# Decoding the first weight matrix without ScalarE and GpSimd, folding key blocks the other way, and a new order of every step

## Chip, cores and metric

The kernel runs on one core of one Trainium2 chip. The metric is device time in microseconds (us) of one execution, lower is better. The engines are TensorE (PE in the rows; PEld is its weight load), VectorE (DVE), ScalarE (ACT), GpSimd (POOL) and SyncE (SP, which here issues nearly all DMAs). Engines run their own queues in order and wait for each other through semaphores.

## The reference

Attention with a sliding window and four sink keys over batch 4, 8 heads, 768 positions and head dimension 64, then a gated layer of width 512 on the joined heads:

```python
scores = (q @ k.T) / sqrt(64)                # per batch and head
keep = (key < 4) | (0 <= query - key < 128)  # sinks, or inside the window
a = softmax(where(keep, scores, -1e9))
x = (a @ v), heads joined to width 512
gate_pre[t] = sum over 5 taps k of conv_w[k] * x[t - 4 + k]
out = (sigmoid(gate_pre) * (x @ w_val)) @ w_out
```

The weights w_val, w_out and conv_w come as float64 and are read as pairs of 32-bit words.

## The kernel before

**Steps of attention.** A step s is one of 24: a batch (4), a third of the positions p (3, 256 queries each) and a half of the heads qd (2). Each step has two units of scores g. `scores` (L376) multiplies 32 queries by the keys of their window in small tiles of TensorE (L396, 64 rows by 32 columns, eight tiles at a time) into one of two pairs of PSUM banks. The keys are laid out in blocks of 64, with the 4 sink keys behind each (HB = 68 columns), and a unit's row holds 200 columns for each of two key positions c: older block, sinks, middle block, sinks, newest block. Since the window is 128 wide, of the older and the newest block exactly one is valid at each place; `copy_predicated` (L401) folds the newest block into the older one's columns, so that the softmax runs over 132 columns instead of 200. For p = 0 the mask of the sequence's start is added while the maximum is taken (L410); for the others a plain maximum (L405) does. `exps` (L414) takes the exponentials on ScalarE, `recip` and `normalise` (L425, L430; five GpSimd operations) divide by the sums, `probs_t` (L449) and `sinks_t` (L462) transpose on TensorE, `probs_x`, `probs_y` and `sinks_e` bring the result to SBUF, `values` and `sinks` (L507, L522) multiply by V into the two banks xv.

**The gated layer.** Every two steps make 256 positions m (12 of them). `x_high`, `x_copy`, `x_low` (L540, L531, L548) split x into a high and a low part; `conv_last` (GpSimd) and `conv` (VectorE, L557, eight operations for each step) add the five taps, `gate` takes the tanh. `val` (L572) multiplies by w_val in three products (L581, 12 matmuls of 256 columns), `gated`, `gated_h`, `gated_l` multiply with the gate and split again, `outp` (L612) multiplies by w_out (L634, 6 matmuls of 512 columns each), `store` and `send` write 128 positions out. For the first m (those under `COPIES`) `val_copy` (L584) copies the product out of its bank to SBUF first, and `gated` reads the copy.

**Decoding of weights.** `_decode` (L124) turns float64 words of one quarter of a matrix (128 x 512) into a high and a low float32 part. `bias`, `bits` and `high` make the high part (ScalarE, VectorE, ScalarE); `power` gives the exponent e (L152, VectorE). `share` scales the low words on ScalarE (L160) and multiplies them by e on GpSimd (L161). `total` adds the three parts on TensorE (L182 to L184), `low` copies the result out (L187). The two last quarters of w_out (`CUT`) take another way.

**Banks.** Two PSUM banks ac (`homes`, L221) serve the decoding, the transposes of the sinks, `val` and `outp` in turn; a step that takes one (`homes.pop`) waits until the step that gave it back has read it. `busy` (L225) is a filler: it multiplies zeros n times in such a bank, so that TensorE works while it has nothing else.

**What sets the order.** `ORDER` (L36) is a table of names, a step's name and its number (s0.4 is unit 0 of the scores of step 4, wvc.0 the third stage of the first quarter of w_val, fill.5 five multiplications of zeros). `banded` runs through it once; the instructions stand on each engine's queue, SP's DMAs too, in exactly that order:

```python
    with tc.manual_schedule():
        for n in ORDER.split():
            f, args = events[n]
            f(*args)
```

The functions that the change touches, as they are in the kernel before:

Of the kernel before, what the change touches and what calls it, by code (L numbers as in the profile page):

```python
# [37 lines left out]
wva.1 kq.1 wvb.1 e0.0 blanks wva.2 wvb.2 vv.0 e1.0 wvf.0 fill.10 s1.1 wvc.2 wvc.1 rec.0 norm.0 wvd.1 e1.1 s0.1
fill.4 fill.7 kq.2 s1.2 wol.0 woa.0 wve.1 sv.0 e0.1 e1.2 wob.0 woc.0 wol.2 tx.0 fill.6 px.0 sk.0 py.0 rec.1
ts.0 wod.0 s0.2 vl.0 woe.0 wvl.3 wva.3 norm.1 wvb.3 kq.3 e0.2 s0.3 wof.0 wvf.1 si.0 xc.0 tx.1 px.1 fill.6 c4.0  # L40
kq.5 wvc.3 rec.2 norm.2 xh.0 wvd.2 hd.0 c0.0 wvd.3 e0.3 wve.2 c1.0 py.1 wol.3 wol.1 woa.1 wve.3 vv.1 wob.1
wvf.3 sv.1 tx.2 py.2 px.2 s1.3 xl.0 sk.1 ts.1 wod.1 wvf.2 kq.4 vl.1 si.1 xc.1 c4.1 sk.2 ts.2 kq.6 hd.1 woc.1
s0.4 xh.1 vv.2 woe.1 c0.1 e1.3 rec.3 woa.3 th.0 vv.5 e0.4 xl.1 v0.0 v1.0 c1.1 y0.0 wob.3 woa.2 norm.3 g0.0
wod.3 h0.0 vl.2 wob.2 th.1 s1.4 e1.4 l0.0 v2.0 v3.0 woe.3 woe.2 y1.0 g1.0 vv.6 tx.3 px.3 si.2 xc.2 hd.2 wof.1
h1.0 s0.6 o2.0 o0.0 rec.4 xh.2 py.3 c4.2 c0.2 l1.0 wof.2 s0.5 c1.2 s1.6 kq.7 wod.2 e0.6 wof.3 o1.0 t0.0 o3.0
norm.4 sk.3 e0.5 vv.3 ts.3 t1.0 xl.2 vl.3 si.3 xh.3 xc.3 hd.3 xl.3 c4.3 sk.4 th.2 s1.5 ts.4 tx.4 sv.6 px.4
e1.5 kq.8 c0.3 scalars d0.0 py.4 rec.5 v0.1 v1.1 y0.1 c1.3 e1.6 rec.6 v2.1 norm.5 g0.1 th.3 h0.1 v3.1 vv.4
y1.1 vl.4 tx.5 d1.0 kq.9 si.4 g1.1 l0.1 px.5 s1.8 sk.5 hd.4 xc.4 ts.5 o0.1 h1.1 c4.4 o2.1 xh.4 c0.4 warm_up
c1.4 py.5 l1.1 e1.8 o3.1 t1.1 s0.7 s1.7 vl.5 xl.4 norm.6 kq.10 tx.6 e0.7 si.5 sk.6 py.6 px.6 ts.6 xc.5 xh.5
o1.1 hd.5 e1.7 xl.5 s0.9 rec.7 t0.1 s0.8 v0.2 c4.5 c0.5 v1.2 th.4 kq.12 g0.2 v2.2 c1.5 e0.9 norm.7 e0.8 rec.8  # L50
sk.7 h0.2 v3.2 l0.2 norm.8 tx.7 ts.7 th.5 g1.2 vl.6 py.7 si.6 px.7 hd.6 h1.2 xc.6 c4.6 l1.2 xh.6 xl.6 s1.9
# [845 lines left out]
```

## Time and profile before

| | before |
|---|---|
| median of 3 runs | 260.79 us (260.79 to 261.36) |
| profiled execution | 260.89 us |
| its span, first to last instruction | 259.1 us |
| PE busy | 251.7 us, 97% |
| PEld busy | 204.2 us, 79% |
| DVE busy | 205.0 us, 79% |
| ACT busy | 187.1 us, 72% |
| POOL busy | 176.9 us, 68% |
| DMA, mean over the span | 141 GB/s |

The span is followed by 1.8 us that no engine's instruction covers. Matmuls are pipelined: a matmul's own duration contains its passage through the array, and what one costs in a row of equals is the distance between two starts. Idle time in a row stands in square brackets behind it, with the engine that ended it. Names are as above: pr the pairs of banks of the scores, ac the two shared banks, xv the banks of values, wv_f and wo_f the scaled low words of w_val and w_out, wx the normalised probabilities, vc the copy that `val_copy` makes.

### The profile page before, as it was taken

The page shows a single profiled execution, that of the slowest core. Times are in us where ns is not written, and L with a number is a line of the kernel's source. Part 1 is how long each engine was busy: PE and PEld are TensorE (multiplying, and loading weights), DVE is VectorE, ACT ScalarE, POOL GpSimd, SP SyncE. Part 2 cuts the span into 40 slices and gives each one's busy share as a digit, 9 for nine tenths or more (in the row PEclk, how much of TensorE's full clock was granted, in tenths as well). Part 3 has the DMA queues.
Part 4 walks back from the last instruction along what each step waited for, and adds up shares of the span by engine and source line. Part 5 has one row for each costly group of instructions (what it writes and reads, how often), then busy time and mean ns, then how long its engine had stood idle before and what let it go on. Part 6 is the DMA issues. An engine that isn't in the chain of part 4 may idle for free.

```text
span 259.1 us, 9951 instructions
## 1 busy us (share of the span) xinstructions
PE 251.7 (97%) x3960; PEld 204.2 (79%) x3964; DVE 205.0 (79%) x561; ACT 187.1 (72%) x692; POOL 176.9 (68%) x241
## 2 busy tenths in 40 slices
PE   8999989999999999999999999999999999999993
PEld 2455559779879878878978879888879898889983
DVE  6976999979889899988987976887778878785610
ACT  3899998979879766897888558583876668444141
POOL 6279897678856991778587675986773659744430
PEclk9999999999999999999999999999999999999999
DMA  6999382356036327908554027274036300520013
GB/s 211 378 333 329 140 259 61 129 159 199 4 106 217 82 82 231 324 4 251 168 156 144 3 65 242 83 233 165 3 104 221 91 4 9 177 83 0 3 61 114
DMA packets 27541, 36.45 MB, mean 141 GB/s; under 512 B 2272, under 2 KB 24032, under 8 KB 27488
## 3 DMA queue, kind: packets, MB, share of 16 engines
q1 hardware_dynamic: 26672, 34.96, 41.9%
q10 hardware_dynamic: 816, 0.79, 1.0%
q8 instruction: 33, 0.54, 0.8%
q14 instruction: 20, 0.16, 0.2%
HBM read 29.45 MB, written 6.29 MB: 138 GB/s over the span
## 4 chain that ended last, share of the span: by engine, by line
PE 84%; ACT 9%; DMA 2%; POOL 2%; DVE 1%; issue 1%
PE ac L581 26%; PE ac L634 22%; PE xv L518 12%; PE pr L396 10%; PE pr L456 5%; ACT w L421 4%; PE pr L634 3%; DMA raw<-in_w_val_dram 2%; PE xv L526 2%; PE ac L464 2%; ACT wv_p L141 1%; ACT wv_p L160 1%; ACT wvl L187 1%; PE ac L630 1%; PE pr L630 1%
## 5 line engine op out<-in xcount | busy, mean ns | idle before, releaser
L562 DVE SCALAR_TENSOR_TENSOR sg<-xv,cw,sg 128x256 f32<-128x256 f32 x192 | 77.8, 473 | 6.9 <-POOL sg L554 6.0
L436 POOL TENSOR_TENSOR wx<-w,sm 128x512 f32<-128x512 f32 x48 | 49.1, 1044 | 2.3 <-DVE sm L428 2.0
L421 ACT ACTIVATE w<-pr,ngm 128x132 f32<-128x132 f32 x136 | 48.5, 369 | 1.7
L581 PE MATMUL ac<-xh,wvh 128*128 128x256 f32 x192 | 48.3, 286 | 0.0
L581 PE MATMUL ac<-xh,wvl 128*128 128x256 f32 x192 | 47.2, 279 | 0.0
L554 POOL TENSOR_TENSOR sg<-xt,cw 128x512 f32<-128x512 f32 x24 | 25.4, 1060 | 29.1 <-ACT xt L533 28.8
L610 POOL TENSOR_TENSOR gl<-sg,gh 128x512 fp32r<-128x512 f32 x24 | 30.8, 1287 | 20.2 <-ACT gh L606 20.2
L581 PEld LDWEIGHTS ac<-xh,wvh 128*128 128x128 f32 x192 | 36.3, 189 | 1.5 <-issue 0.8
L581 PEld LDWEIGHTS ac<-xh,wvl 128*128 128x128 f32 x192 | 36.1, 188 | 0.3
L396 PE MATMUL pr<-k,q 64*32 64x168 f32 x1536 | 35.5, 307 | 0.2 <-DVE wt L487 0.2
L518 PE MATMUL xv<-wt,v 64*64 64x192 f32 (+2 forms) x1024 | 34.5, 278 | 0.2 <-ACT wt L495 0.2
L518 PEld LDWEIGHTS xv<-wt,v 64*64 64x64 f32 x1024 | 30.4, 133 | 5.1 <-issue 1.2
L634 PE MATMUL ac<-woh,gh 128*128 128x512 f32 x80 | 33.4, 417 | 0.0
L549 POOL TENSOR_TENSOR xl<-xt,xh 128x512 fp32r<-128x512 f32 x24 | 30.8, 1287 | 3.8 <-ACT xh L541 2.6
L634 PE MATMUL ac<-woh,gl 128*128 128x512 f32 x80 | 31.7, 396 | 0.0
L634 PE MATMUL ac<-wol,gh 128*128 128x512 f32 x80 | 31.6, 396 | 0.0
L581 PE MATMUL ac<-xl,wvh 128*128 128x256 f32 x192 | 30.2, 279 | 0.0
L396 PEld LDWEIGHTS pr<-k,q 64*32 64x32 f32 x1536 | 23.5, 106 | 7.6 <-issue 2.4
L401 DVE COPY_PREDICATED pr<-low,pr 128x256 f32<-128x256 uint8 x48 | 20.2, 422 | 11.3 <-PE pr L396 9.0
L421 ACT ACTIVATION_READ_ACCUMULATOR w<-pr,ngm 128x1 f32 x136 | 27.6, 203 | 0.0
L581 PEld LDWEIGHTS ac<-xl,wvh 128*128 128x128 f32 x192 | 25.8, 188 | 0.0
L405 DVE TENSOR_REDUCE ngm<-pr 128x4 f32<-128x528 f32 x34 | 24.0, 707 | 1.2
(156 smaller groups left out, 482.0 us busy)
## 6 DMA issues: line engine op xcount, KB each, us to landing
k<-in_kt_dram SPq DMA_DIRECT2D x23, 408.0 KB, 4.7
v<-in_vt_dram SPq DMA_DIRECT2D x16, 384.0 KB, 4.0
q<-in_qt_dram SPq DMA_DIRECT2D x23, 256.0 KB, 5.2
out_dram<-osb SPq DMA_DIRECT2D x23, 256.0 KB, 3.6
v<-in_vt_dram SPq DMA_DIRECT2D x8, 256.0 KB, 4.1
raw<-in_w_out_dram SPq DMA_DIRECT2D x4, 512.0 KB, 7.5
raw<-in_w_val_dram SPq DMA_DIRECT2D x3, 512.0 KB, 6.0
raw<-in_w_val_dram ACTq DMA_DIRECT2D x1, 512.0 KB, 4.8
```

Of the source, the lines that this page charges most:

```text
L396: nc.tensor.matmul(ss[e * QB:(e + 1) * QB, j, c * n + x0:c * n + x1], q[js, g, (4 * c + e) * QB:(4 * c + e + 1) * QB], k[js, g, (2 * c + e ...
L401: nc.vector.copy_predicated(sv[:, :, :, :D], low[:, None, None, :].to_broadcast([P, 2, 2, D]), sv[:, :, :, 2 * HB:])
L405: nc.vector.tensor_reduce(out=ngm[:, g], in_=sv[:, :, :, :PK], axis=mybir.AxisListType.X, op=ALU.max)
L421: nc.scalar.activation(out=w[:, g, j, c], in_=sx[:, j, c, :PK], func=AF.Exp, scale=0.125 if whole else -1.0, bias=ngm[:, g, j, c:c + 1], a ...
L436: nc.gpsimd.tensor_tensor(out=t[:, n].rearrange("p c h x -> p h c x"), in0=w[:, :, :, at], in1=sm.to_broadcast([P, 4, 2, D]), op=ALU.mult)
L518: nc.tensor.matmul(acc[o * D:(o + 1) * D, g, x0 + h * D:x0 + (h + a1 - a0 + 1) * D], v[js, g, n], t[js, n % 2, n // 2, g, a0:a1 + 1].rearr ...
L549: nc.gpsimd.tensor_tensor(out=half(xls, s, "xl", F32R), in0=xts[s], in1=half(xhs, s, "xh", F32R).bitcast(F32), op=ALU.subtract)
L554: nc.gpsimd.tensor_tensor(out=half(sg, s, "sg", F32), in0=xts[s], op=ALU.mult, in1=cw[:, g, KT - 1:].to_broadcast([P, 2, PQ]))
L562: nc.vector.scalar_tensor_tensor(out=g, in0=x, scalar=a, in1=g, op0=ALU.mult, op1=ALU.add)
L581: nc.tensor.matmul(acc[:, h], a[:, kc, cs], x[:, kc], start=(n == 0), stop=(n == 11))
L610: nc.gpsimd.tensor_tensor(out=gl, in0=g, in1=gh.bitcast(F32), op=ALU.subtract)
L634: nc.tensor.matmul(acc, a[:, kc, ts], x[:, kc], start=(kc + n == 0), stop=(kc + n == 5))
```

## The change

Four edits and a new table.

1. **Low words in one operation.** For the four quarters of w_val (`DIR`) one VectorE operation reads the raw low words, scales them and multiplies them by e. The ScalarE and the GpSimd operation of `share` go for these quarters; w_out keeps them.
2. **Fold the other way.** The older block is folded into the newest block's columns where the older one is valid (`high` is the opposite mask of `low`), and all that follows reads columns 68 to 200 instead of 0 to 132. At the start of the sequence (p = 0, c = 0) there is no older block: its columns are neither multiplied nor folded.
3. **Masks.** The masks of `masks` and `leads` move to the new columns; `leads` builds one part by a VectorE copy in place of four GpSimd memsets.
4. **No copies.** `COPIES` is 0: the four `val_copy` go, and `gated` reads the bank itself.
5. **Order.** All lines of `ORDER` are new. The fillers are the same number (38) in six groups: 5, 10, 4, 7, 6, 6 before; 6, 10, 4, 6, 7, 5 now.

```diff
 ORDER = """
-masks load_conv wvl.0 signs kq.0 leads conv_weights fill.5 wva.0 wvb.0 wvd.0 s0.0 wvl.1 s1.0 wvc.0 wve.0 wvl.2
...
+load_conv masks wvl.0 kq.0 signs leads conv_weights wva.0 wvl.1 wvl.2 wvb.0 wvd.0 fill.6 wva.1 s0.0 e0.0 s1.0
+kq.1 fill.10 kq.2 wvc.0 wva.2 wvb.1 blanks vv.0 wol.0 fill.4 wve.0 wvb.2 e1.0 wvd.1 s1.1 rec.0 wvf.0 s0.1
...
+DIR = (("wv", 0), ("wv", 1), ("wv", 2), ("wv", 3))
 MP = 10
 LAST = (B * NP - 1, 1)
-COPIES = 2
+COPIES = 0
...
     def share():
 
-        if not cut:
+        if direct:
+            nc.vector.scalar_tensor_tensor(out=f, in0=lo.bitcast(U32), scalar=2.0 ** -52, in1=ef, op0=ALU.mult,
+                                           op1=ALU.mult)
+        elif not cut:
             nc.scalar.activation(out=pf, in_=lo.bitcast(U32), func=AF.Copy, scale=2.0 ** -52)
             nc.gpsimd.tensor_tensor(out=f, in0=ef, in1=pf, op=ALU.mult)
...
-        lo, hi = slice(0, D), slice(D, P)
-        nc.gpsimd.memset(lead, 0.0)
-        nc.gpsimd.memset(lead[:, 0, :D], -BIG)
...
+        nc.gpsimd.memset(lead[:, 0, :HB], 0.0)
+        nc.gpsimd.memset(lead[:, 1], 0.0)
+        nc.gpsimd.memset(lead[:D, 1, :NSK], -BIG)
+        nc.vector.tensor_copy(out=lead[:, 0, HB:], in_=mask[:, 0])
...
                     x0, x1 = (e % 2) * QB, n - QB + (e % 2) * QB
+                    if p + c == 0:
+                        x0, x1 = HB, n
                     nc.tensor.matmul(ss[e * QB:(e + 1) * QB, j, c * n + x0:c * n + x1],
...
-        nc.vector.copy_predicated(sv[:, :, :, :D], low[:, None, None, :].to_broadcast([P, 2, 2, D]),
-                                  sv[:, :, :, 2 * HB:])
+        c0 = 0 if p else 1
+        nc.vector.copy_predicated(sv[:, :, c0:, 2 * HB:], high[:, None, None, :].to_broadcast([P, 2, 2 - c0, D]),
+                                  sv[:, :, c0:, :D])
+        sv = sv[:, :, :, HB:]
```

What the table and the edits make of the queues is seen at three places. On **GpSimd near the start**, from the blanks of the sinks (skb) on; wv_f and wo_f are the products of `share`, wx and skb those of `normalise`, vh the sinks' values. Before:

```order
L338 MEMSET skb_107 128x128
L338 MEMSET skb_108 128x128
L161 TENSOR_TENSOR wv_f<-wv_e,wv_p 128x512 x2
L436 TENSOR_TENSOR wx<-w,sm 128x4x2x64 x2
L440 TENSOR_TENSOR skb_107<-w,sm 128x2x16
L443 TENSOR_SCALAR skb_107<-skb_107 128x2x16
L444 TENSOR_TENSOR skb_107<-skb_107 128x2x16
L264 TENSOR_TENSOR vh<-vs,vh 16x128 x2
L161 TENSOR_TENSOR wo_f<-wo_e,wo_p 128x512
L436 TENSOR_TENSOR wx<-w,sm 128x4x2x64 x2
```

and in the change:

```order
L339 MEMSET skb_107 128x128
L339 MEMSET skb_108 128x128
L442 TENSOR_TENSOR wx<-w,sm 128x4x2x64 x2
L446 TENSOR_TENSOR skb_107<-w,sm 128x2x16
L449 TENSOR_SCALAR skb_107<-skb_107 128x2x16
L450 TENSOR_TENSOR skb_107<-skb_107 128x2x16
L268 TENSOR_TENSOR vh<-vs,vh 16x128 x2
L442 TENSOR_TENSOR wx<-w,sm 128x4x2x64 x2
L446 TENSOR_TENSOR skb_108<-w,sm 128x2x16
L449 TENSOR_SCALAR skb_108<-skb_108 128x2x16
L450 TENSOR_TENSOR skb_108<-skb_108 128x2x16
L165 TENSOR_TENSOR wo_f<-wo_e,wo_p 128x512
```

The products of w_val are gone, and the first wo_f now stands behind the second `normalise` instead of ahead of it.

On **VectorE near the start**, behind the second quarter's first operations; pr_86 and pr_87 are the pairs of banks. Before:

```order
L401 COPY_PREDICATED pr_87<-low,pr_87 128x2x2x64
L405 TENSOR_REDUCE ngm<-pr_87 128x4
L144 TENSOR_SCALAR wv_t<-wv_p 128x512
L146 SCALAR_TENSOR_TENSOR wv_t<-wv_p,wv_t 128x512
L152 TENSOR_SCALAR wv_e<-wv_t 128x512
```

and in the change:

```order
L406 COPY_PREDICATED pr_87<-high,pr_87 128x2x64
L411 TENSOR_REDUCE ngm<-pr_87 128x4
L161 SCALAR_TENSOR_TENSOR wv_f<-raw,wv_e 128x512
L145 TENSOR_SCALAR wv_t<-wv_p 128x512
L147 SCALAR_TENSOR_TENSOR wv_t<-wv_p,wv_t 128x512
L153 TENSOR_SCALAR wv_e<-wv_t 128x512
```

The fold is half as wide for these units of p = 0, and the new operation stands between the scores and the next quarter.

On **SP at the end**, the last stores; 128x512 is a store of 128 positions, 128x256 one of the two halves of the last. Before:

```order
L661 DMA out_dram<-osb 128x512 x3
L645 DMA out_dram<-osb 128x256 x2
```

and in the change:

```order
L667 DMA out_dram<-osb 128x512 x2
L651 DMA out_dram<-osb 128x256
L667 DMA out_dram<-osb 128x512
L651 DMA out_dram<-osb 128x256
```

One whole store now stands between the two halves.

## Rows read from the trace of the kernel before

**Rows 1.** Busy time by engine before and after PE's first product with w_val: stretch, length, PE, PEld, DVE, ACT, POOL, PEclk, DMA, GB/s.

```profile
6.30:37.83 31.53, 29.36 (x465) 16.50 (x467) 27.57 (x70) 30.08 (x114) 23.70 (x32) 1.00 0.85 286
37.83:255.10 217.27, 217.26 (x3486) 185.95 (x3484) 173.58 (x468) 154.15 (x574) 149.00 (x188) 1.00 0.38 119
```

**Rows 2.** Waits of PE, whole span: us in total, times, longest.

```profile
PE ac L184 <- POOL wo_f L161: 0.7, 1, 0.7
PE pr L456 <- ACT w L421: 0.4, 1, 0.4
...
PE pr L396 <- DVE wt L487: 0.2, 1, 0.2
```

**Rows 3.** Timeline of PE to its first product with w_val: start, duration, instruction.

```profile
3.72 2.34 PE L228 MATMUL ac<-zero 128*128 128x512 bf16 x5
...
6.49 0.80 PE L396 MATMUL pr<-k,q 64*32 64x168 f32 x32
...
14.01 2.55 PE L228 MATMUL ac<-zero 128*128 128x512 bf16 x10
...
17.21 1.13 PE L182 MATMUL ac<-wv_t,ident 128*128 128x512 f32 x2
...
18.73 0.71 PE L456 MATMUL pr<-ident,wx 64*128 64x64 f32 x16
...
27.47 1.02 PE L182 MATMUL ac<-wv_t,ident 128*128 128x512 f32 x2
```

**Rows 4.** Chain of waits, 60 to 100 us: start, duration, what.

```profile
67.55 4.21 PE ac L634 x18
71.75 1.30 PE pr L396 x64
...
84.90 1.14 PE xv L518 x32
...
87.65 4.39 PE ac L634 x18
...
92.69 0.73 PE pr L396 x32
```

**Rows 5.** Lines L160 and L161, the two operations of `share`: durations minimum/median/maximum in ns.

```profile
L160 ACT ACTIVATE wv_p<-raw x4: 672/695/701, 8.0 to 26.6; 128x512 f32<-128x512 uint32 x4
...
L161 POOL TENSOR_TENSOR wv_f<-wv_e,wv_p x4: 1270/1277/1290, 8.8 to 27.8; 128x512 fp32r<-128x512 f32 x4
```

**Rows 6.** Line L146, the nearest operation of VectorE to the new one.

```profile
L146 DVE SCALAR_TENSOR_TENSOR wv_t<-wv_p,wv_t x4: 691/691/692, 6.8 to 25.2; 128x512 int32<-128x512 int32 x4
```

**Rows 7.** Line L600, `gated`, from a bank and from a copy.

```profile
L600 DVE SCALAR_TENSOR_TENSOR sg<-sg,ac x20: 634/680/689, 81.7 to 246.8; 128x512 f32<-128x512 f32 x20
...
L600 DVE SCALAR_TENSOR_TENSOR sg<-sg,vc x4: 684/726/1410, 41.7 to 66.1; 128x512 f32<-128x512 f32 x4
```

**Rows 8.** Timelines of POOL and DVE about the slowest of those four.

```profile
65.67 1.27 POOL L610 TENSOR_TENSOR gl<-sg,gh 128x512 fp32r<-128x512 f32 x1
...
66.08 1.41 DVE L600 SCALAR_TENSOR_TENSOR sg<-sg,vc 128x512 f32<-128x512 f32 x1 [1.18 <-ACT vc L587]
```

**Rows 9.** Timeline of POOL, 0 to 42 us.

```profile
16.70 2.05 POOL L436 TENSOR_TENSOR wx<-w,sm 128x512 f32<-128x512 f32 x2
...
20.49 0.96 POOL L264 TENSOR_TENSOR vh<-vs,vh 16x128 fp32r<-16x128 f32 x2
21.60 1.27 POOL L161 TENSOR_TENSOR wo_f<-wo_e,wo_p 128x512 fp32r<-128x512 f32 x1 [0.15 <-POOL vh L264]
```

**Rows 10.** Timeline of DVE: fold of one unit of p = 0, and the reciprocal behind its maxima.

```profile
13.61 0.43 DVE L401 COPY_PREDICATED pr<-low,pr 128x256 f32<-128x256 uint8 x1 [0.21 <-PE pr L396]
...
14.94 0.20 DVE L428 RECIPROCAL sm<-sm 128x8 f32<-128x8 f32 x1
```

**Rows 11.** Timeline at the end: the last part of a store and its DMA.

```profile
255.13 0.38 ACT L643 ACTIVATE osb<-ac 128x256 f32<-128x256 f32 x1 [0.98 <-PE ac L630]
255.54 0.52 SPq L645 DMA_DIRECT2D out_dram<-osb  x1
```

More of the change, by code (lines that the diff above doesn't have):

```diff
@@ L36 @@
 ORDER = """
-masks load_conv wvl.0 signs kq.0 leads conv_weights fill.5 wva.0 wvb.0 wvd.0 s0.0 wvl.1 s1.0 wvc.0 wve.0 wvl.2
[L38 to L51, printed above, removed]
@@ new lines @@
+kq.1 fill.10 kq.2 wvc.0 wva.2 wvb.1 blanks vv.0 wol.0 fill.4 wve.0 wvb.2 e1.0 wvd.1 s1.1 rec.0 wvf.0 s0.1
+wvd.2 fill.6 scalars e1.1 norm.0 s1.2 e0.1 wvc.2 sv.0 fill.7 rec.1 kq.3 wvl.3 vv.1 tx.0 wol.2 wvc.1 wve.1 sk.0
+woa.0 px.0 e1.2 py.0 wob.0 s0.2 ts.0 s0.3 wvf.1 norm.1 woc.0 vl.0 wod.0 woe.0 wva.3 e0.2 si.0 wvb.3 tx.1 rec.2
+xc.0 wof.0 hd.0 xh.0 wvd.3 c4.0 wvc.3 fill.5 px.1 c0.0 wol.1 e0.3 norm.2 kq.4 wve.2 c1.0 wvf.2 wve.3 woa.1
+sv.1 wob.1 sk.1 py.1 tx.2 ts.1 py.2 xl.0 woc.1 vl.1 wod.1 wvf.3 si.1 px.2 kq.5 s1.3 sk.2 xc.1 wol.3 xh.1 hd.1
@@ new lines @@
+ts.2 s0.4 c4.1 woe.1 xl.1 v0.0 woa.2 c0.1 th.0 woa.3 e1.3 v1.0 vv.2 c1.1 g0.0 rec.3 th.1 wob.2 s1.4 woe.2 h0.0
+vl.2 norm.3 e0.4 e1.4 v2.0 kq.6 wob.3 kq.7 v3.0 tx.3 wof.1 g1.0 si.2 px.3 woe.3 s0.5 l0.0 xc.2 sk.3 rec.4 vv.3
+h1.0 hd.2 ts.3 wof.2 py.3 c4.2 xh.2 wod.3 o2.0 o0.0 c0.2 wod.2 vv.6 c1.2 e0.5 l1.0 s0.6 wof.3 o3.0 o1.0 s1.6
+norm.4 vl.3 kq.8 th.2 t1.0 xl.2 si.3 xh.3 xc.3 t0.0 xl.3 s1.5 c4.3 d1.0 hd.3 sk.4 tx.4 px.4 e1.5 c0.3 ts.4
+rec.5 v0.1 norm.5 v1.1 e0.6 v2.1 py.4 e1.6 c1.3 g0.1 v3.1 th.3 h0.1 vv.4 g1.1 l0.1 s1.8 vl.4 tx.5 rec.6 px.5
@@ new lines @@
+c1.10 v2.4 v3.4 warm_up norm.12 g0.4 tx.12 g1.4 vv.13 norm.13 th.10 kq.15 py.12 h0.4 si.11 vl.11 px.12 s0.14
+s1.14 sk.12 l0.4 h1.4 xc.11 o2.4 hd.11 ts.12 l1.4 e0.18 c4.11 o3.4 xl.10 o0.4 c0.11 e0.14 d0.2 o1.4 kq.19
+e1.14 vv.14 c1.11 tx.13 px.13 xh.11 rec.14 si.12 t1.4 py.13 t0.4 s1.18 kq.17 vl.12 hd.12 xl.11 sv.13 xc.12
+xh.12 s1.15 s0.15 d1.3 e1.15 vv.19 sk.13 ts.13 v0.5 v1.5 c4.12 th.11 v2.5 norm.14 c0.12 e0.15 g0.5 sv.19 kq.16
+v3.5 c1.12 tx.14 g1.5 h0.5 si.13 h1.5 vl.13 vv.15 l0.5 px.14 sk.14 o0.5 xc.13 l1.5 py.14 hd.13 xh.13 s0.16
@@ L121, in _flag, with _decode @@
     nc.vector.tensor_copy(out=flag_i, in_=flag[:, 2:3])
-def _decode(nc, pool, raw, n, whi, wlo, shape, unit=None, bank=None, eng=None):
+def _decode(nc, pool, raw, n, whi, wlo, shape, unit=None, bank=None, eng=None, direct=False):
     lo, hi = raw[..., 0], raw[..., 1]
@@ L268, in banded @@
     d, d0, c4, t0, t1 = (mk[:, n] for n in range(5))
-    low = cn.tile([P, D], U8, name="low")
+    high = cn.tile([P, D], U8, name="high")
     cur = cn.tile([P, D], F32, name="cur")
@@ L283, in masks @@
         nc.vector.tensor_copy(out=d[:, :D], in_=ti[0])
-        nc.vector.tensor_scalar(out=low, in0=d[:, :D], scalar1=0.0, scalar2=None, op0=ALU.is_ge)
+        nc.vector.tensor_scalar(out=high, in0=d[:, :D], scalar1=0.0, scalar2=None, op0=ALU.is_lt)
         nc.vector.tensor_copy(out=d0[:, :D], in_=ti[1])
@@ L356, in decode_weights @@
             dec[n, c] = _decode(nc, p2, raws[n, c], n, *hl, [P, 4, P] if n == "wv" else [P, DM],
-                                (ident, plus, minus), None if (n, c) in CUT else homes, nc.gpsimd if (n, c) in PWR else nc.vector)
+                                (ident, plus, minus), None if (n, c) in CUT else homes, nc.gpsimd if (n, c) in PWR else nc.vector,
+                                (n, c) in DIR)
         dec[n, c][stage]()
```

75 lines of the change are left out of this document (35 added, 40 removed).

## Prediction

> **What bounds the kernel.** The first view is busy time by engine, cut where TensorE begins its first product with w_val, at 37.83 us [rows 1]. Behind that cut TensorE is busy 217.26 of 217.27 us, while VectorE has 44 us to spare there, ScalarE 63 and GpSimd 68. Ahead of it TensorE is idle 2.2 us of 31.5, and the fullest engine is ScalarE (30.1), then VectorE (27.6). A busy TensorE can hide stalls, since durations overlap, so the second view is the chain of waits [rows 4]: from 37.99 us to 255.11 it holds TensorE's groups alone, and equal groups take equal time, 0.73 for every lone unit of scores, for instance. The third view, TensorE's waits, has none behind 37.5 us; those ahead of it are small [rows 2]. So the time is: the start (37.8), then TensorE's work without a gap (217.3), then the tail, from TensorE's end to the end of the span (4.0), and 1.8 around the span. An edit on another engine pays only in the start, or if it makes TensorE wait where it doesn't now.
>
> **TensorE's own work behind the cut.** Same matmuls in the same numbers, but for one edit: the scores of p = 0, c = 0 are 132 columns wide instead of 168. One unit alone takes 0.73 and two in a row 1.30 [rows 4], so a unit's own work is 0.57 for 168 + 168 columns of each small tile, 1.70 ns a column. 36 columns fewer are 0.061 a unit. There are 16 such units (8 steps, two units), 4 of them in the start: 12 x 0.061 = **-0.73**. Bounds: 0, if the issue of the 32 instructions set the pace, and -0.73; I take the upper, as 0.57 is nearest to the columns' sum.
> The order changes how often TensorE goes from one tile shape to another. One such change costs 0.16 between lone units of scores (0.73 - 0.57), and (4.39 - 4.21) = 0.18 for two sides of a group of 18 products [rows 4], so about 0.1 each. Counting in the table from v0.0 on, there were 102 changes and are now 105: **+0.3**.
> Both together: -0.4.
>
> **The start.** The edit of the low words takes from ScalarE four operations of 0.70 (0.58 from one start to the next) and from GpSimd four of 1.28, 5.1 in all [rows 5], and gives VectorE four. The nearest row is the other operation with two sources in SBUF, 0.69 [rows 6]; the upper bound is 1.41 [rows 7], of which more below. I take 0.69: 2.8 more on VectorE, less 0.2 for each half fold of the 4 early units (0.43 whole [rows 10]), so +2.0 against 4.0 of idle time there [rows 1]. TensorE gets the same 38 fillers, so it can gain no more than its waits. I follow the chain that the new order gives:
> - The sixth filler stands ahead of the first scores, where a filler takes 0.43 (2.34 for five with the last one's passage) [rows 3]: s0.0 starts at 6.9 instead of 6.49. Two units and their masks take 1.9 as now: 8.8. Fourteen fillers (10 now take 2.47 with their edges, 0.22 for each more) 3.3, and a decode 1.5 (17.21 to 18.73) [rows 3]: s1.1 at 13.6, done at 14.3.
> - On VectorE rec.0 now stands behind that unit: the half fold and four masked maxima (13.61 to 14.94 now [rows 10], 0.2 less): the reciprocal is ready at 15.6.
> - GpSimd starts `normalise` of step 0 at 15.7, a microsecond earlier than now (16.70), since no wv_f stands ahead of it; but wo_f.0 has moved behind the next `normalise`. 3.7 + 1.0 + 3.7 + 1.3 [rows 9]: wo_f.0 at 25.4, where it now is at 22.9.
> - TensorE from 14.3: one unit, six fillers, one unit, seven fillers, transposes, decode, sinks, two units, values, and two of the three parts of woe.0: 0.6 + 1.5 + 0.7 + 1.75 + 0.7 + 1.5 + 0.3 + 1.3 + 1.15 + 1.1 gives 24.9. It waits 0.5 for wo_f.0, ends that part at 25.8, and si.0, tx.1 and five fillers (0.3 + 0.65 + 1.2) bring wve.2 to 28.0, half a microsecond later than now (27.47).
> - What is left until v0.0 is the same work: 37.83 - 27.47 - 1.3 of waits [rows 2] = 9.1. The waits should go: GpSimd, without wv_f.3, has wo_f.1 at 35.2 when TensorE asks at 36.4 (now it is 0.7 late), the low part of x at 37.6 for 38.0, and VectorE has its part of woe.1 at 32.7 for 35.
> v0.0 comes at 37.1: **-0.8** (37.83 - 37.05).
>
> **What is moved beside it.** Without the copies, four ScalarE operations go, and the banks of m = 0 and 1 come free only when VectorE has gated them. The tightest is o2.0, 1.6 behind v3.0, while `gated` takes 0.68 [rows 7] behind 0.5 of decoding: it fits, 0. Raw words of w_val are now read by VectorE and not ScalarE, so their buffers come free about 4 us later (18.9 instead of 14.6); SP's queue stands there with two loads of w_out and what is behind them (keys and queries of step 4). These land by 28, and are read at 31 and later: 0. On SP, near the end, V of step 23 now stands behind three stores and is issued some 2 us after o1.9; 8.4 of TensorE's work lie in between, so 2 are left when it lands in 4: 0. The check of the scalars (2.5 on VectorE) moves ahead of a bank's release near 220 us with 0.2 to spare: I take +0.1. At the tail a store of 128 positions is issued between the halves of the last one; the last half waits for ScalarE until 255.5 anyway [rows 11], so it costs at most one issue (0.5): I take **+0.1**.
>
> **Sum.** -0.4 - 0.8 + 0.1 + 0.1 = -1.0 against the profiled execution's 260.89: 259.9. The median of the runs is 260.79, 0.1 below it, so I forecast **259.8**. Differences under 0.3% (0.8 us) count as none here: faster is under 260.0, slower over 261.6. My forecast's own spread (chain +-0.5, bank +0.3) is 259.3 to 260.4, and two thirds of it lie under 260.0.
>
> **A rule that speaks against the change.** In the copy form of `gated`, one of four took 1.41 instead of 0.69: it began at 66.08 beside a GpSimd operation and was let go about when that ended, at 66.94 [rows 8]. The 20 that read one source from a bank never passed 0.69 [rows 7]. The Trainium skill says the same in SBUF — State Buffer, section Who interferes with whom: a VectorE instruction with two inputs in SBUF shares its second read port with GpSimd, and whoever issues first blocks the other. The trace agrees. By the row alone, the new operation can take 1.41 as well as 0.69. By 0.69 the start's sum is the one above; by 1.41 it is the second rival's.
>
> **Rivals.**
> - *Only TensorE is left in the start* (0.22). wo_f.0 comes in time, if GpSimd runs 0.5 ahead of my chain (its 3.7 for a `normalise` holds small gaps). The 0.5 of waiting goes, and the first scores lose only 0.2. For: ScalarE, fullest in the start, loses 2.3. Against: the new place of wo_f.0. v0.0 at 36.3, -1.5 - 0.4: 258.9.
> - *VectorE sets the start* (0.12, slower). Each new operation waits behind GpSimd: 4 x 1.41 - 0.8 = +4.8 of VectorE, and its idle time ahead of the cut is 4.0 [rows 1], of which a part waits for scores and can't be filled. With all of it filled v0.0 is 0.9 later, with half 2.8; minus 0.4, plus 0.2: 261.6 to 263.5, I take 262.3. It decides from 1.2 an operation on. Against: at two of the four places GpSimd has nothing to run.
> - *No gain in the start* (0.15). Another wait takes the place of those removed, for instance `exps` of step 1, which now waits for s1.1 behind 14 fillers. -0.4 + 0.1: 260.5.
> - *The narrow scores don't shorten a unit* (0.06), because instructions and not columns set 0.57: 260.6.
>
> **How the numbers follow.** The forecast has 0.45. Faster: two thirds of it and the first rival, 0.52; within 0.3%: the rest of it and the last two, 0.36; slower: 0.12. The range 258.4 to 261.5 leaves out most of the slower rival and the low end of the first.
>
> **What the profile will show.** First product with w_val near 37.0; TensorE's longest wait for wo_f at woe.0, none at woe.1; L161 on VectorE at 0.69 four times (over 1.2 speaks for the second rival). Lone units of p = 0 at 0.67 instead of 0.73. Behind the first product no wait over 0.3: one there, at a bank, at the transposes or at the values of step 23, would prove me wrong, as would a tail over 4.3.

## The result: slower by 1.1%, and the profile after

The changed kernel takes 264.01 us (median of 4 runs, 263.71 to 264.14) where the one before takes 260.99 (median of 4): a ratio of 1.0112, 95% interval 1.0100 to 1.0124. The forecast was 259.8, the range 258.4 to 261.5. One execution of experiment 10 (286.67 us) and one of the kernel before beside it (306.63) ran at a lower granted clock (0.85 and 0.76); ratios leave them out, medians do not.

| | before | after |
|---|---|---|
| profiled execution | 260.89 us | 263.89 us |
| its span | 259.1 us | 262.0 us |
| first product with w_val | 37.83 us | 38.79 us |
| from there to TensorE's end | 217.26 us | 218.65 us |
| from there to the end of the span | 4.0 us | 4.5 us |

Busy time of the kernel after by stage, cut at the first product with w_val and at 57.94 us, behind TensorE's last wait (columns as in [rows 1]):

```profile
6.00:38.79 32.79, 28.93 (x467) 16.47 (x467) 30.90 (x72) 28.10 (x103) 19.09 (x29) 1.00 0.80 270
38.79:57.94 19.15, 17.69 (x268) 13.88 (x267) 18.91 (x37) 13.96 (x55) 14.48 (x17) 1.00 0.25 76
57.94:257.40 199.46, 199.43 (x3218) 171.69 (x3218) 155.46 (x434) 138.86 (x522) 134.75 (x172) 1.00 0.40 122
```

The third column of busy time is VectorE's. Ahead of the cut it is now the fullest engine (30.9 of 32.8 us, where it had 27.6 of 31.5 [rows 1]), and in the 19 us behind it, it is idle for 0.24 us. From 57.94 us on TensorE never waits again, as before. Its waits in the kernel after (us in total, times, longest), to be laid beside [rows 2]:

```profile
...
PE xv L524 <- DVE sg L568: 1.1, 1, 1.1
PE pr L400 <- ACT wo_p L164: 1.0, 1, 1.0
PE ac L188 <- POOL wo_f L165: 0.9, 1, 0.9
PE ac L640 <- DVE sg L606: 0.8, 1, 0.8
PE ac L640 <- POOL wol L177: 0.5, 1, 0.5
PE pr L400 <- ACT w L427: 0.4, 1, 0.4
...
```

(Left out are the 1.2 us ahead of TensorE's first multiplication, which every run here has, and waits of 0.3 or less.) The first three and the last lie in the start, the two at L640 behind it. Two more go back to VectorE, under another engine's name: the scores that start at 36.62 need banks that VectorE had read out at 36.52 (L493 at 35.84, 0.68; ScalarE's wo_p had been done since 35.65), and GpSimd's wol was waiting for VectorE's L173, until 53.56. In whole: +0.96 until the first product, +1.45 of waits behind it (0.81, 0.49, and 0.15 at a bank), -0.06 of TensorE's own work, +0.5 at the tail: 2.9, the difference of the spans.

Why VectorE is late is seen in its timeline. L147 is the operation that was L146 in the kernel before, and took 0.69 there in all eight quarters, four of them in [rows 6]:

```profile
20.93 1.41 DVE L147 SCALAR_TENSOR_TENSOR wo_t<-wo_p,wo_t 128x512 int32<-128x512 int32 x1
22.38 1.15 DVE L153 TENSOR_SCALAR wo_e<-wo_t 128x512 int32<-128x512 int32 x1
27.30 1.49 DVE L161 SCALAR_TENSOR_TENSOR wv_f<-raw,wv_e 128x512 fp32r<-128x512 uint32 x1
33.22 1.64 DVE L147 SCALAR_TENSOR_TENSOR wo_t<-wo_p,wo_t 128x512 int32<-128x512 int32 x1
...
42.99 1.41 DVE L147 SCALAR_TENSOR_TENSOR wo_t<-wo_p,wo_t 128x512 int32<-128x512 int32 x1
...
47.32 1.65 DVE L147 SCALAR_TENSOR_TENSOR wo_t<-wo_p,wo_t 128x512 int32<-128x512 int32 x1
48.90 0.68 DVE L606 SCALAR_TENSOR_TENSOR sg<-sg,ac 128x512 f32<-128x512 f32 x1
...
51.32 1.51 DVE L171 TENSOR_SCALAR wo_f<-raw 128x512 int32<-128x512 int32 x1
```

and GpSimd's at the same places (x2 is a pair of operations in a row):

```profile
20.69 2.55 POOL L442 TENSOR_TENSOR wx<-w,sm 128x512 f32<-128x512 f32 x2
...
27.20 1.04 POOL L560 TENSOR_TENSOR sg<-xt,cw 128x512 f32<-128x512 f32 x1 [1.63 <-ACT xt L539]
...
32.96 1.36 POOL L555 TENSOR_TENSOR xl<-xt,xh 128x512 fp32r<-128x512 f32 x1
...
42.75 2.56 POOL L442 TENSOR_TENSOR wx<-w,sm 128x512 f32<-128x512 f32 x2 [3.24 <-DVE sm L434]
...
46.97 1.46 POOL L616 TENSOR_TENSOR gl<-sg,gh 128x512 fp32r<-128x512 f32 x1
...
51.08 1.48 POOL L616 TENSOR_TENSOR gl<-sg,gh 128x512 fp32r<-128x512 f32 x1
```

At all seven of VectorE's slow operations GpSimd's had begun first. At 33.22, 47.32 and 51.32, each beside a single one of GpSimd, VectorE's ended 0.54, 0.54 and 0.27 us after GpSimd's, a little under its own duration undisturbed (0.69, 0.69, 0.43). These seven operations of VectorE lost 0.7 to 1.1 us each, 6.0 in all, until 57.94 us; in the kernel before, two operations lost 0.4 and 0.5 up to there. Only one of the seven is the new operation; of its four, three took 0.64 to 0.70:

```profile
L161 DVE SCALAR_TENSOR_TENSOR wv_f<-raw,wv_e x4: 640/691/1490, 9.9 to 27.3; 128x512 fp32r<-128x512 uint32 x4
```

At the end of SP's queue, the stores behind [rows 11] (L667 the whole one, L651 the halves):

```profile
256.52 0.33 SPq L651 DMA_DIRECT2D out_dram<-osb  x1
256.91 1.17 SPq L667 DMA_DIRECT2D out_dram<-osb  x1
258.17 0.38 SPq L651 DMA_DIRECT2D out_dram<-osb  x1
```

ScalarE had the last half ready at 257.86, and SP issued it 0.3 later, since the whole store's issue took 1.17. The span then ends 3.8 us behind the start of that last issue, where the kernel before needs 3.6 from 255.54 on [rows 11]. So of the 0.5 by which the tail grew, 0.3 is the late issue, and the rest comes after it.

### The profile page after: what moved, and what is told of

It reads as the page before. It is cut to its first block, busy times and chain, and to the rows that moved or that the text cites. A ratio compares the mean times of both kernels' runs of the same rounds, so it can differ in the third digit from the quotient of the medians.

```text
span 262.0 us, 9930 instructions
## 1 busy us (share of the span) xinstructions
PE 250.9 (96%) x3961; PEld 203.8 (78%) x3964; DVE 209.2 (80%) x566; ACT 183.7 (70%) x684; POOL 171.8 (66%) x234
## 4 chain that ended last, share of the span: by engine, by line
PE 85%; DVE 7%; ACT 4%; issue 2%; POOL 0%; DVEq 0%; ACTq 0%
PE ac L587 26%; PE ac L640 20%; PE xv L524 12%; PE pr L400 10%; PE pr L462 5%; PE pr L640 3%; ACT w L427 3%; PE ac L470 2%; PE xv L532 2%; DVE sg L568 1%; PE ac L232 1%; DVE wt L493 1%; PE ac L186 1%; PE pr L217 1%; DVE wo_t L147 1%
## 5 line engine op out<-in xcount | busy, mean ns | idle before, releaser
L442 POOL TENSOR_TENSOR wx<-w,sm 128x512 f32<-128x512 f32 x48 | 50.6, 1073 | 20.5 <-DVE sm L434 20.3
L616 POOL TENSOR_TENSOR gl<-sg,gh 128x512 fp32r<-128x512 f32 x24 | 31.0, 1298 | 18.9 <-ACT gh L612 18.8
L400 PE MATMUL pr<-k,q 64*32 64x168 f32 (+1 forms) x1536 | 34.0, 302 | 1.4 <-ACT wo_p L164 1.0
L640 PE MATMUL ac<-woh,gh 128*128 128x512 f32 x80 | 33.2, 415 | 0.8 <-DVE sg L606 0.8
L640 PE MATMUL ac<-wol,gh 128*128 128x512 f32 x80 | 31.7, 397 | 0.5 <-POOL wol L177 0.5
L640 PE MATMUL ac<-woh,gl 128*128 128x512 f32 x80 | 31.7, 396 | 0.0
L427 ACT ACTIVATION_READ_ACCUMULATOR w<-pr,ngm 128x1 f32 x136 | 27.6, 203 | 0.0
L406 DVE COPY_PREDICATED pr<-high,pr 128x256 f32<-128x256 uint8 (+1 forms) x48 | 18.1, 378 | 8.1 <-PE pr L400 6.2
```

Of the source, the lines that this page charges most:

```text
L400: nc.tensor.matmul(ss[e * QB:(e + 1) * QB, j, c * n + x0:c * n + x1], q[js, g, (4 * c + e) * QB:(4 * c + e + 1) * QB], k[js, g, (2 * c + e ...
L406: nc.vector.copy_predicated(sv[:, :, c0:, 2 * HB:], high[:, None, None, :].to_broadcast([P, 2, 2 - c0, D]), sv[:, :, c0:, :D])
L427: nc.scalar.activation(out=w[:, g, j, c], in_=sx[:, j, c, :PK], func=AF.Exp, scale=0.125 if whole else -1.0, bias=ngm[:, g, j, c:c + 1], a ...
L442: nc.gpsimd.tensor_tensor(out=t[:, n].rearrange("p c h x -> p h c x"), in0=w[:, :, :, at], in1=sm.to_broadcast([P, 4, 2, D]), op=ALU.mult)
L616: nc.gpsimd.tensor_tensor(out=gl, in0=g, in1=gh.bitcast(F32), op=ALU.subtract)
L640: nc.tensor.matmul(acc, a[:, kc, ts], x[:, kc], start=(kc + n == 0), stop=(kc + n == 5))
```

## Experiments

"New table" and "old table" are the two values of `ORDER`. Ratios are to the kernel before in the same batch of runs, with their 95% intervals; times are medians. Experiments 1 to 4, 5 to 8 and 9 to 12 are three batches on three chips, so runs of different batches are compared by their ratios.

**1. The new table without VectorE's new operation.**

```diff
-DIR = (("wv", 0), ("wv", 1), ("wv", 2), ("wv", 3))
+DIR = ()
```

> The new table and all edits but one: the low words of w_val go through ScalarE and GpSimd again. Theory 1 (VectorE is the bound from 17 to 57 us, by its four new operations of 0.68 to 1.49 us and by waiting beside GpSimd): VectorE has 3.5 us less to do, so the first product with w_val comes at 37.3 to 38.2 us instead of 38.79, the stalls of 0.8 and 0.5 us near 49 and 55 us shrink to under 0.5 together, and the time falls from 264.0 to 262.0 to 263.2. Theory 2 (the table's places on GpSimd decide, the products behind normalise above all): GpSimd has 5.1 us more to do in places made without them, the waits for its wo_f grow to 1.5 us or more, and the time is 264.0 to 266.

268.95 us, ratio 1.030 (1.026 to 1.034). Theory 2 was the nearer one, and worse than it said. GpSimd makes the second and third product of w_val behind its first normalise, the third here:

```profile
22.71 1.32 POOL L165 TENSOR_TENSOR wv_f<-wv_e,wv_p 128x512 fp32r<-128x512 f32 x1
```

and TensorE waits 2.54 us for it:

```profile
24.09 0.50 PE L188 MATMUL ac<-wv_f,plus 128*128 128x512 f32 x1 [2.54 <-POOL wv_f L165]
```

The first product comes at 43.02 us. So with this table the new operation isn't what costs: it saves some 5 us, a part of them by the clock, which is at 0.69 of full speed from 26 to 30 us, behind that wait. Nor is it what brings the blocking: without it six of VectorE's decoding operations still lose 0.5 to 1.1 us each beside GpSimd. The run doesn't tell what VectorE's 2.8 us would be worth elsewhere, since GpSimd and ScalarE became the bound.

**2. The new table with the four copies.**

```diff
-COPIES = 0
+COPIES = 2
-v0.0 woa.2 ... v1.0 vv.2
+v0.0 woa.2 ... v1.0 y0.0 vv.2
```

(y1.0, y0.1 and y1.1 likewise, each behind its v.)

> The new table and all edits, but the four copies of val's product are back, each right behind its val. Theory A (a bank that VectorE frees late is a delay of its own): TensorE's wait of 0.8 us for VectorE's gated at 49 us goes and the time falls to 263.2. Theory B (VectorE is in arrears as a whole): the 0.8 us go there and come back at the next place, where TensorE waits for the low part of w_out that hangs on VectorE too: that wait grows from 0.5 to 1.0 us or more, and the time is 263.7 to 264.1.

265.77 us, 1.016 (1.013 to 1.019): both theories fell short. The 0.8 us for gated goes, and a wait of 2.03 us takes its place, at 52.02, at the other bank: ScalarE frees it (skt, L478) behind its part of the gate, and that stands behind VectorE's gated, which reads two sources in SBUF again and was let go about when GpSimd's product (48.40, 1.74) ended:

```profile
48.91 1.77 DVE L606 SCALAR_TENSOR_TENSOR sg<-sg,vc 128x512 f32<-128x512 f32 x1
```

TensorE also waits 0.62 us at 73 us for GpSimd's product (gl, L616), which it doesn't in the changed kernel. The wait of 2.03 cost more than itself. By stage (columns as above), PEclk is 0.50 for the three microseconds that follow, TensorE's lower level of 1.2 GHz, after two in which it did nothing:

```profile
50.00:52.00 2.00, 0.00 (x0) 0.00 (x0) 2.00 (x4) 1.28 (x5) 2.00 (x3) 1.00 0.00 0
53.00:56.00 3.00, 3.00 (x37) 1.63 (x37) 2.93 (x8) 1.79 (x7) 1.75 (x2) 0.50 0.00 0
57.00:60.00 3.00, 3.00 (x63) 2.09 (x65) 2.90 (x14) 1.16 (x3) 2.54 (x5) 1.00 0.03 5
```

**3. The whole store ahead of the two halves.**

```diff
-d0.11 o2.11 o3.11 d1.10 t1.11
+d0.11 d1.10 o2.11 o3.11 t1.11
```

> Only the store of 128 positions that stands between the two halves of the last one is moved ahead of them. Theory A (its issue on SP delays the last half): the end of the span comes 0.5 us earlier behind TensorE's end (4.0 instead of 4.6 us), 263.5. Theory B (the landing of all the stores sets it): no difference, 264.0.

262.50 us, 1.0055 (1.0036 to 1.0075); the changed kernel run again (experiment 5) has 1.0088 (1.0069 to 1.0107). Theory A: SP issues the last half as ScalarE ends, and the span ends 3.4 us behind TensorE. The size is loose, as the other profiles with the stores in this order end 4.0 to 4.5 us behind TensorE, those with the new order 4.5 to 4.7: some 0.4 us, and what the medians differ beyond that isn't explained by the store.

**4. The fold alone, in the old table.**

```diff
-DIR = (("wv", 0), ("wv", 1), ("wv", 2), ("wv", 3))
+DIR = ()
-COPIES = 0
+COPIES = 2
```

(`ORDER` as before. This diff and those of 11 and 12 are against the changed kernel.)

> The old table with the fold the other way alone (the scores of p = 0, c = 0 are 132 columns wide; the copies and ScalarE's and GpSimd's low words stay). Theory A (the columns set what a unit costs): 12 units behind the first product with w_val are 0.06 us shorter, TensorE needs 216.5 us from there to its end instead of 217.2, and the time is 260.0 to 260.4. Theory B (32 instructions set it): 261.0.

260.64 us, 0.9981 (0.9970 to 0.9992). Between the theories, nearer to A: TensorE needs 216.80 us from its first product with w_val instead of 217.26, 0.46 less. In the chain of waits the five lone units of p = 0 behind the cut take 0.67 instead of 0.73, and the five pairs that hold the other seven 1.24 to 1.29 instead of 1.30 to 1.38, for example:

```profile
116.28 0.67 PE pr L400 x32
119.24 1.26 PE pr L400 x64
```

So the 0.06 are there for a lone unit, 0.30 in all. The five pairs are left with 0.16 of the 0.46 together, where 7 x 0.061 would be 0.43.

**5. The changed kernel again**, with no edit.

> The changed kernel itself once more, beside the others on their chip, since single times of the new table have lain up to 2.4 us apart. 263.5 to 264.2; the first product with w_val at 38.1 to 38.8 us, and the same three blocked operations of VectorE between 42 and 52 us.

263.67 us, 1.0088 (1.0069 to 1.0107); the first product comes at 38.47, and the same seven operations of VectorE are blocked, with the same durations within 0.01 us. What varies is when the start gets there: with the queues unchanged up to 30 us, the profiles of experiments 2, 3 and 9 have the first product at 38.24, 38.09 and 38.28, the one of the result at 38.79.

**6. One GpSimd step away from one VectorE step.**

```diff
-py.2 xl.0 woc.1 vl.1
+py.2 woc.1 xl.0 vl.1
```

> One step of the new table is moved: the low part of x of step 0 goes behind the product for w_out's second quarter, so GpSimd has nothing to run while VectorE runs L147 near 33 us. Theory 1 (that operation is blocked by GpSimd's, and VectorE is the bound): L147 takes 0.69 us instead of 1.65, TensorE's wait of 1.0 us for the scores' banks behind it goes, and the first product with w_val comes 0.7 to 1.0 us earlier than in the kernel with the new table as it is; the time falls by 0.3 to 1.0 us. Rival (the operation is slow by itself, or something else holds the scores): L147 stays at 1.65 us or the first product stays where it is; no difference in time.

263.42 us, 1.0094 (1.0073 to 1.0114). In the trace theory 1 holds, but not in the time:

```profile
32.94 0.69 DVE L147 SCALAR_TENSOR_TENSOR wo_t<-wo_p,wo_t 128x512 int32<-128x512 int32 x1
```

TensorE's 1.0 us for the scores' banks is gone, and the first product comes at 37.56, 0.91 earlier than in experiment 5 and 0.5 earlier than in any other profile with the table as it was up to there. But the time stays within the interval. TensorE then waited 0.45 for the low part of x, which the move makes later; conv of step 1 waited 0.62 for GpSimd, whose steps came later by the move, and the same three operations were blocked behind 42 us, so that gated, at 48.39 instead of 48.58, freed TensorE's bank only 0.2 earlier:

```profile
49.12 0.50 PE L640 MATMUL ac<-woh,gh 128*128 128x512 f32 x1 [0.86 <-DVE sg L606]
```

**7. All edits of the code with the old table.**

```diff
-v1.0 ... y0.0 g0.0
+v1.0 ... g0.0
```

(The code is that of the changed kernel; `ORDER` is the one before, without y0.0, y1.0, y0.1 and y1.1.)

> All edits of the code with the old table (without the four copies). Theory 1 (the edits load VectorE, where the old table has no room either: 16.8 of 17.2 us behind the first product with w_val): slower than the fold alone (260.6) by over 1 us, 261.7 to 264, with waits for VectorE near 48 us. Theory 2 (the table is what costs): 259.5 to 260.7, the first product with w_val no later than 37.8 us.

260.45 us, 0.9971 (0.9957 to 0.9985). Theory 2: the edits make the kernel faster, and the table makes it slower by 3 us. VectorE's eight operations L147 take 0.69 to 0.83 there, with the same work on both engines, and of all its decoding only two operations lose more than 0.3 (0.35 and 0.54), where seven lost 6.0 with the new table. Theory 1 saw one thing rightly, the bank that is free too late without copies:

```profile
PE ac L640 <- DVE sg L606: 0.8, 1, 0.8
PE ac L188 <- DVE wv_f L161: 0.7, 1, 0.7
PE pr L400 <- DVE wt L493: 0.7, 1, 0.7
```

(The profiled execution took 261.49 us, the longest of the ten, so its waits may be longer than those of most.)

**8. The blocking by itself, in the kernel before.**

```diff
-wva.1 kq.1 wvb.1 e0.0 blanks wva.2 wvb.2
+wva.1 kq.1 wvb.1 e0.0 blanks probe wva.2 wvb.2
...
+    extra = [cn.tile([P, 512], F32, name=f"extra{n}") for n in range(2)]
+
+    def probe():
+        nc.gpsimd.memset(extra[0], 1.0)
+        for _ in range(2):
+            nc.gpsimd.tensor_tensor(out=extra[1], in0=extra[0], in1=extra[0], op=ALU.mult)
...
```

> The kernel before, with a fill and two products of 128 x 512 from SBUF added on GpSimd from 10.4 to 13.4 us, where it has nothing to run; nobody reads them. Theory 1 (GpSimd and VectorE keep each other out while an operation reads SBUF twice): of VectorE's two operations L146 of that time (0.69 us each) one or both take 1.2 us or more, or GpSimd's products take over 1.6 us where VectorE was first. Rival (the long durations of the new table have another cause, such as DMA traffic or PSUM): 0.69 us, and 1.27 us on GpSimd. The time itself changes by under 0.5 us.

Theory 1. GpSimd:

```profile
10.18 0.54 POOL L337 MEMSET extra<- 128x512 f32 x1
10.79 2.54 POOL L339 TENSOR_TENSOR extra<-extra 128x512 f32<-128x512 f32 x2
```

VectorE, the first three operations beside it, the last three (the same for the next quarter) behind it:

```profile
9.91 1.08 DVE L144 TENSOR_SCALAR wv_t<-wv_p 128x512 int32<-128x512 int32 x1
11.03 1.40 DVE L146 SCALAR_TENSOR_TENSOR wv_t<-wv_p,wv_t 128x512 int32<-128x512 int32 x1
12.47 1.15 DVE L152 TENSOR_SCALAR wv_e<-wv_t 128x512 int32<-128x512 int32 x1
13.54 0.42 DVE L144 TENSOR_SCALAR wv_t<-wv_p 128x512 int32<-128x512 int32 x1
13.98 0.69 DVE L146 SCALAR_TENSOR_TENSOR wv_t<-wv_p,wv_t 128x512 int32<-128x512 int32 x1
14.78 0.43 DVE L152 TENSOR_SCALAR wv_e<-wv_t 128x512 int32<-128x512 int32 x1
```

The three operations take 1.08, 1.40 and 1.15 beside GpSimd and 0.42, 0.69 and 0.43 without it; the first three took 0.63, 0.69 and 0.43 in the kernel before, for the same quarter. That the time changes by under 0.5 doesn't fit the one execution there is: with 2.1 us more on VectorE the first product comes at 39.07 instead of 37.83, and the time is 262.96, where the kernel before has 261.29.

**9. The exponentials and the reciprocal of step 3 earlier.**

```diff
-xl.1 v0.0 woa.2 c0.1 th.0 woa.3 e1.3 v1.0 vv.2 c1.1 g0.0 rec.3 th.1
+xl.1 e1.3 v0.0 woa.2 c0.1 rec.3 th.0 woa.3 v1.0 vv.2 c1.1 g0.0 th.1
```

> In the new table the exponentials of step 3 and the reciprocal behind them come earlier on ScalarE and VectorE (the reciprocal between the two halves of conv, as in the old table), so that GpSimd's normalise of step 3 runs beside conv, which reads a bank, and no longer beside VectorE's two operations L147 of 1.41 and 1.65 us at 42 to 49 us. Theory (these two are blocked, and with them the bank that TensorE waits for): at least one of the two falls to 0.69 to 0.9 us, TensorE's wait of 0.8 us near 49 us falls to under 0.4, and the time by 0.3 to 1.0 us, to 262.8 (ratio to before 1.005 to 1.008, against 1.009 of the new table as it is). Rival (VectorE is simply full there): the waits keep their sum of 1.3 us, no difference.

262.94 us, 1.0060 (1.0041 to 1.0078). One of the two operations fell from 1.41 to 0.69, as expected, since normalise now runs beside conv; the other did not, since GpSimd's wol (46.75, 1.39) has taken the place of gl beside it. So the bank is as late as before (0.93), but VectorE is 0.6 ahead behind it, and the wait of 0.5 for wol is gone:

```profile
42.90 0.69 DVE L147 SCALAR_TENSOR_TENSOR wo_t<-wo_p,wo_t 128x512 int32<-128x512 int32 x1
...
47.04 1.65 DVE L147 SCALAR_TENSOR_TENSOR wo_t<-wo_p,wo_t 128x512 int32<-128x512 int32 x1
48.61 0.67 DVE L606 SCALAR_TENSOR_TENSOR sg<-sg,ac 128x512 f32<-128x512 f32 x1
```

**10. The moves of 3, 6 and 9 together.**

```diff
-py.2 xl.0 woc.1 vl.1
+py.2 woc.1 xl.0 vl.1
-xl.1 v0.0 woa.2 c0.1 th.0 woa.3 e1.3 v1.0 vv.2 c1.1 g0.0 rec.3 th.1
+xl.1 e1.3 v0.0 woa.2 c0.1 rec.3 th.0 woa.3 v1.0 vv.2 c1.1 g0.0 th.1
-d0.11 o2.11 o3.11 d1.10 t1.11
+d0.11 d1.10 o2.11 o3.11 t1.11
```

> The new table with three moves: the low part of x of step 0 behind the product for w_out, the exponentials and the reciprocal of step 3 earlier, and the whole store ahead of the halves of the last one. Theory: the gains add: 0.3, 0.3 to 1.0 and 0.9 us, 261.3 to 262.2 (ratio to before 1.000 to 1.004). Rival (each gain is given back at the next operation that VectorE is late with): over 262.6.

261.41 us, 1.0006 (0.9986 to 1.0026): the gains add, and the moves take back nearly the whole loss against the kernel before. Measured one by one they lower the ratio by 0.0055 together (experiments 3, 6 and 9, against 5), here by 0.0082; each ratio is known to some 0.002. The first product comes at 37.23, and TensorE's waits for VectorE fall from 1.1, 1.0 (through ScalarE) and 0.8 to these:

```profile
PE xv L524 <- DVE wo_t L145: 0.3, 1, 0.3
...
PE ac L640 <- DVE sg L606: 0.3, 1, 0.3
```

Not all of this profile is owed to the moves. The new operation near 27 us isn't blocked here, and no move stands ahead of it in any queue:

```profile
27.13 0.69 DVE L161 SCALAR_TENSOR_TENSOR wv_f<-raw,wv_e 128x512 fp32r<-128x512 uint32 x1
...
27.14 1.58 POOL L560 TENSOR_TENSOR sg<-xt,cw 128x512 f32<-128x512 f32 x1 [2.07 <-ACT xt L539]
```

VectorE came first by 0.01 us. In the six other profiles of the new table with this operation GpSimd came first by some 0.1, and it took 1.49 or 1.50. How often that falls out so in the executions without a profile isn't known; the nine fast ones lie between 260.22 and 262.20 us.

**11. The old table, the fold and the new operation, with copies.**

```diff
-COPIES = 0
+COPIES = 2
```

(`ORDER` as before.)

> The old table with the fold and the low words on VectorE, and with the four copies. Theory (without copies TensorE waits 0.8 us at 48 us for gated in the old table too; with them the bank is free in time): that wait goes, 259.6 to 260.1, the fastest so far. Rival (gated from a copy reads SBUF twice, is blocked by GpSimd, and what it delays is as late): 260.3 to 260.9, as all edits with the old table.

260.29 us, 0.9951 (0.9934 to 0.9969), the lowest ratio of all, though the interval overlaps that of experiment 7. The time lies above the theory's range and at the edge of the rival's, but in the trace the theory holds: the wait of 0.8 at 48 us is gone, and from its first product (37.50 us) to its end TensorE is idle for 0.07 us in all. The two largest left are in the start:

```profile
PE ac L188 <- DVE wv_f L161: 1.0, 1, 1.0
PE pr L400 <- DVE wt L493: 0.7, 1, 0.7
```

**12. The new operation for one quarter of w_out alone.**

```diff
-DIR = (("wv", 0), ("wv", 1), ("wv", 2), ("wv", 3))
+DIR = (("wo", 1),)
-COPIES = 0
+COPIES = 2
```

(`ORDER` as before.)

> The old table with the fold and the copies; the low words go to VectorE for one quarter alone, the second of w_out, whose product on GpSimd TensorE waits 0.7 us for just ahead of its first product with w_val. Theory: that wait goes and nothing takes its place, the first product at 37.1 us instead of 37.8, 259.9 to 260.2. Rival (VectorE, full from 38 to 55 us, carries the 0.7 us on to a bank): first product earlier, but a wait near 48 us, 260.5 or more.

261.74 us, 1.0017 (1.0007 to 1.0027): the rival, at another bank. The first product does come at 37.15 us; but the operation was itself blocked (at 35.73, 1.03 us instead of 0.69), conv behind it was a microsecond late, and TensorE waited for the bank that it reads, in a place where it hadn't waited before:

```profile
41.14 1.55 PE L524 MATMUL xv<-wt,v 64*64 64x64 f32 x48 [1.03 <-DVE sg L568]
```

## Why the prediction was wrong

**What bounds the kernel.** Right from 58 us on: TensorE runs through, and a difference there is one of its own work alone. Wrong from 38 to 58 us: the view was cut at 37.83, and "VectorE has 44 us to spare" is the sum over 217 us [rows 1], wherever in them it lies. The kernel before has VectorE idle for only 0.35 us of the 17 that follow:

```profile
37.83:55.00 17.17, 17.17 (x272) 14.14 (x271) 16.82 (x44) 14.58 (x53) 13.18 (x14) 1.00 0.40 121
```

That stretch should have had a row of its own.

**TensorE's own work.** The mechanism was right, the term mis-sized: -0.73 for the narrow units is -0.46 (experiment 4), since the seven units that stand in pairs gain 0.16 together and not 0.43. With the changes of tile shape, put at +0.3, the measured sum is -0.06 in place of -0.4; by difference these cost +0.4.

**The start.** The chain holds to 28 us: wo_f.0 was forecast for 25.4 and ended at 25.57, wve.2 for 28.0 and began at 28.18. The step that failed is the next one, "What is left until v0.0 is the same work" and "The waits should go": VectorE's part of woe.1, forecast for 32.7, was ready at 35.3, and TensorE waited 1.07 and 0.99 us. -0.8 became +0.96. The forecast of 37.05 isn't far from what the table gives once blocked operations are apart: 37.56 in experiment 6, and 37.23 in experiment 10, where the chance at 27.13 has a part in it.

**The rule that speaks against the change.** It was read rightly and applied to one operation only. I priced the new operation at 0.69 or at 1.41 and left every other operation of VectorE at its duration in the kernel before; but the table had moved all of them, and GpSimd's too. The new operation was blocked once in four times (+0.8), the decoding of w_out, which the edits don't touch, six times (+5.2). Two of these six have a single source (L153, L171), which the rule as the prediction put it doesn't cover. So the second rival had the mechanism (VectorE sets the start, since it waits beside GpSimd) with a chance of 0.12, but its own condition, all four new operations at over 1.2, did not come about. It also ended at v0.0, where the blocked operations go on to 52 us.

**What is moved beside it.** "It fits, 0" for the bank at o2.0 is wrong by 0.8 us. A wait there is seen with the old table too (experiment 7), and the copies remove it there (experiment 11): 0.68 for gated and 0.5 for a decode left no room for a decode of 1.65 ahead of gated. In the old table one decode is slowed ahead of it, by 0.54 at 40.43 us, and VectorE has no gap from there to gated at 47.61; of the wait of 0.76 in that profile the rest, some 0.2, is a VectorE that is full without blocking. The stall of 0.5 for wol wasn't foreseen at all. A wait over 0.3 at a bank was named as what would prove the forecast wrong, as was a tail over 4.3, and both came. The +0.1 for the check of the scalars did not: TensorE has no wait behind 57.94 us.

**The tail.** It grew by 0.5, the bound named for one issue, not by the 0.1 taken. The issue of a whole store between two halves took 1.17 us, where I priced it by a half's (0.52 [rows 11]), and that made the last issue 0.3 late. That the sum meets the bound of 0.5 is luck: the other 0.2 came behind the last issue and was no part of the reasoning.

**What the change does, split.** By the ratios of experiments 7 and 11 the edits with the old table make the kernel 0.8 to 1.3 us faster, of which the fold alone has 0.5 (experiment 4); the new table costs 3.2 on top of experiment 7 (263.67 against 260.45). Shown is that VectorE is blocked with the new table and hardly with the old one, and that moving four steps takes back some 2.1 of the 3.2 (ratio 1.0088 to 1.0006, experiment 10). How much of these 2.1 is the blocking and how much the order of the stores isn't separated. Of the 1.1 left, 0.4 may be the changes of tile shape, which no run tries alone; four decoding operations are still blocked in experiment 10 (1.19 to 1.65 us each), and what they cost isn't split further.

## What to carry to other kernels

Before an order is changed, lay the operations of VectorE that have no source in a PSUM bank and those of GpSimd side by side in time, for every place that moves, and price each pair that comes to overlap at about the sum of both durations (0.69 and 1.36 took 1.90 from 32.96 us on), not only the operations that an edit adds. Where the two begin within 0.1 us of each other, price both outcomes, since either may come first. A stretch in which an engine is idle for 2% carries any delay on to its end, so look for such stretches in windows of 10 to 20 us (here 0.35 of 17); the share over the whole span hides them. And test the code and the order apart: here the edits were worth a gain that the order lost several times over.

## What the runs showed of the hardware

- VectorE and GpSimd block each other also where VectorE's operation has a single source: 128 x 512 int32 TENSOR_SCALAR took 1.15 (L153), 1.51 (L171) and, in experiment 8, 1.08 and 1.15 us beside GpSimd, 0.43 without it. conv and gated, with one source in a bank, kept their durations beside GpSimd (gated took 0.63 to 0.69 in all 24 cases, the one at 48.90 beside GpSimd's from 48.38 to 50.11 among them). The Trainium skill, in SBUF — State Buffer, section Who interferes with whom, says that VectorE's tensor_scalar can run in a mode that takes both of its ports, and that whoever issues first then blocks the other for the whole instruction. The traces agree.
- GpSimd pays as well where VectorE is first: its pair of products in normalise took 2.49 to 2.56 us where one of VectorE's slow or decoding operations was running as it began, and 2.05 [rows 9] else. In experiment 10 VectorE came first by 0.01 us: GpSimd's product took 1.58 instead of 1.04, VectorE's operation 0.69 instead of 1.50.
- After 2.03 us without work TensorE's granted clock was 0.50 (1.2 GHz) from 53 to 56 us, and 512-column matmuls, 0.23 from start to start at 1.00, took 0.43 there (experiment 2). The kernel after has no such stretch: its waits of up to 1.1 us left the clock at 1.00.
- The issue of a store of 128 positions on SP took 0.33 us with nothing just ahead of it and 1.17 to 1.38 between two halves, in the six profiles with that order.
